# One instruction order exchanged for another in a transformer block written out by hand

## The chip, the cores and the metric

The kernel runs on one core of a Trainium2 chip. A core has a matrix engine (TensorE, PE in the profile), a vector engine (VectorE, DVE), a scalar engine (ScalarE, ACT), a small general one (GpSimd, POOL) and SyncE (SP), which here only starts transfers. Each engine works through its own list of instructions in order; between engines they wait on semaphores. On-chip memory is SBUF, and PE writes into eight PSUM banks. The metric is the device time in microseconds; three runs of the kernel before gave 239.56, 240.42 and 240.76, median 240.42.

## The reference

One block of a diffusion transformer, 2048 rows of 512 channels in bf16: a layer norm scaled and shifted by a condition, an attention in which each row sees itself and seven earlier rows two apart, a gate, and a gated feed-forward (FFN) with 1792 hidden channels.

```python
mod = (silu(c) @ w_mod).reshape(1, 6, 1, 512)
sa, ca, ga, sb, cb, gb = mod's six rows
h = layernorm(x) * (1 + ca) + sa
x = x + ga * A(h)
h = layernorm(x) * (1 + cb) + sb
x = x + gb * B(h)

def A(x):                     # 32 heads of 16, window 8, dilation 2
    q, k, v = split(x @ wqkv)
    idx = pos[:, None] - 2 * arange(8)[None, :]
    logits = einsum('bhsd,bhswd->bhsw', q, k[idx]) * 0.25    # idx < 0 masked
    return einsum('bhsw,bhswd->bhsd', softmax(logits), v[idx]) @ wo

def B(x):
    return (silu(x @ w1) * (x @ w3)) @ w2
```

## The kernel before, in words

The rows are 16 tiles T of 128. The kernel first builds a list of 1151 operations in the order of the mathematics (`_build`), each with its engine, what it reads and writes, and a key such as ("av", 3). Three tables then fix the program: `ORDER` (L1018), a permutation of the 1151 numbers; `SLOTS` (L1064), which gives each temporary value its buffer; and `place` (L147), which deals the operations of `ORDER` out to the engines, each engine keeping the sequence in which its own appear. A value that takes a buffer over also waits for all users of the one before it. `synchronize` (L169) puts the semaphore waits in and `emit` (L212) writes the five lists. So nothing is scheduled while it runs: an engine whose next instruction waits holds everything behind it. This holds for SP too, which starts nearly all transfers (L127, one line for all).

What the operations are, by line:

- **Start.** Fifteen matmuls on a tile of ones (L542) keep PE busy while loads arrive. The condition's first two rows come from matmuls with one column (L514, L517) on w_mod, which is loaded in four pieces of 256 KB: scale columns (operations 24, 25), then shift columns (26, 27). The k weights are operations 31 and 32. A small load of the w_mod corner (20) goes through ACT's queue.
- **Layer norm 1** in groups of tiles [0, 1], [2, 3], [4 to 7], [8 to 11], [12 to 15]: statistics on DVE (L580), the power -0.5 on POOL, for tiles 8 to 15 a bias on DVE (L591) and the normalising on ACT. The transposing is done by PE (L663, evicted by ACT L673), for the last group by DMA (`ln_T`, L633).
- **q, k, v.** Matmuls L722 and L749; ACT evicts them (L730, L734, L759). Each v tile goes through one of six buffers to the DRAM scratch `v_scratch_dram`.
- **Attention of a tile.** DVE multiplies q with eight shifted keys (L780, 128x4096, into a buffer of the pool "big": `sb_pq` or `sb_vsh`, later also `sb_vshx`, `sb_vshq`). PE sums over channels (L791). DVE and ACT do the softmax (L803, L808, L821, L833 to L840; L840 is a transposition on DVE). Four loads (L855) bring the shifted values from the scratch into another "big" buffer, DVE weights them (L862), PE sums over the window (L871), ACT evicts (L877), a DMA transposes (L878), PE multiplies with wo (L895) and DVE adds the residual (L899).
- **FFN** in groups of tiles [0, 1], [2, 3], [4 to 7], [8 to 11], [12 to 15], numbered 0 to 4. Layer norm 2 (`ln_sums`): mean on DVE (L610), squares on ACT (L614), POOL (L620, L621), bias on DVE (L622), normalising on ACT (L625). For groups 2 to 4 four DMA transposes (L644) and four ACT instructions (L648) then make the input h. Fourteen units of hidden channels follow, each two half units of PE (L911: w1, then w3), SiLU on ACT (L917), a copy on ACT (L921) and a product on DVE (L922), or for the last group DVE alone (L925). Then w2 (L953, L941), the residual on DVE (L969) and the store.

Weights are loaded in parts: four of w1, w3 and w2 each (operations 46 to 57; 49 is the second of w3, 54 the first of w2). The attention of later tiles is interleaved with FFN units of earlier groups, so that PE and DVE work side by side.

Of the kernel before, what the change touches and what calls it, by code (L numbers as in the profile page):

```python
# [280 lines left out]
def _build(p, A_x, A_wqkv, A_wo, B_w1, B_w3, B_w2, c, w_mod, out):  # L281
# [737 lines left out]
    15, 20, 1, 5, 7, 8, 16, 6, 17, 4, 2, 21, 58, 3, 22, 23, 28, 24, 25, 31, 32, 10, 11, 12, 13, 14, 0, 63, 64, 65, 66, 67, 87, 88, 89, 59,  # L1019
    60, 90, 68, 69, 70, 71, 92, 93, 91, 94, 61, 72, 62, 101, 19, 95, 161, 73, 163, 78, 74, 75, 79, 76, 96, 164, 162, 165, 80, 97, 102, 98,  # L1020
    77, 99, 103, 105, 115, 116, 120, 121, 106, 100, 166, 104, 107, 108, 168, 26, 81, 122, 123, 167, 169, 173, 27, 170, 82, 84, 83, 171, 174,
    176, 172, 18, 110, 127, 111, 117, 118, 125, 112, 113, 128, 126, 85, 86, 119, 124, 33, 149, 34, 35, 29, 36, 30, 37, 211, 219, 43, 38,
    212, 209, 150, 151, 217, 155, 156, 152, 157, 175, 158, 159, 153, 109, 114, 9, 180, 181, 154, 41, 49, 210, 192, 129, 195, 186, 187, 160,
    44, 198, 130, 201, 182, 218, 40, 144, 405, 220, 265, 188, 145, 45, 267, 42, 266, 139, 202, 203, 146, 147, 213, 183, 184, 140, 185, 196,
    197, 199, 404, 148, 141, 221, 193, 194, 131, 132, 133, 134, 200, 416, 214, 215, 216, 226, 225, 222, 224, 228, 223, 227, 230, 189, 177,
    233, 232, 231, 178, 234, 276, 413, 229, 274, 277, 268, 235, 415, 236, 325, 377, 142, 205, 206, 135, 179, 275, 414, 332, 334, 136, 137,
    333, 403, 190, 191, 406, 249, 251, 143, 378, 247, 253, 138, 323, 278, 269, 270, 271, 279, 273, 324, 272, 289, 280, 281, 285, 282, 207,
    208, 262, 263, 264, 248, 284, 392, 394, 393, 39, 283, 290, 291, 395, 425, 286, 287, 292, 250, 288, 294, 326, 327, 239, 240, 293, 204,
    396, 335, 397, 398, 54, 252, 243, 241, 242, 423, 237, 238, 254, 245, 295, 314, 399, 384, 259, 336, 400, 337, 338, 340, 339, 328, 401,
    297, 343, 329, 330, 341, 331, 402, 385, 417, 260, 261, 303, 299, 379, 315, 301, 380, 305, 300, 342, 52, 407, 302, 244, 246, 381, 344,  # L1030
    426, 418, 424, 304, 408, 419, 454, 420, 317, 296, 409, 427, 428, 256, 382, 386, 309, 306, 410, 320, 456, 318, 429, 430, 257, 421, 310,
    347, 422, 411, 431, 457, 455, 345, 307, 412, 639, 311, 346, 348, 387, 359, 640, 641, 642, 485, 436, 312, 643, 361, 432, 351, 446, 308,
    360, 363, 644, 646, 383, 437, 444, 298, 362, 652, 645, 255, 365, 651, 321, 653, 433, 647, 353, 447, 487, 258, 352, 354, 648, 650, 445,
    649, 371, 448, 372, 654, 368, 369, 449, 488, 450, 435, 434, 438, 486, 439, 440, 458, 459, 50, 47, 51, 316, 460, 357, 358, 355, 489, 490,
    366, 356, 491, 705, 707, 374, 364, 708, 516, 492, 493, 46, 670, 494, 313, 53, 700, 375, 715, 716, 451, 452, 453, 441, 442, 443, 733,
    349, 671, 48, 461, 462, 717, 388, 706, 350, 734, 660, 477, 735, 463, 709, 701, 718, 719, 55, 736, 737, 465, 468, 672, 467, 370, 464,
# [73 lines left out]
```

## Time and profile before

| | us |
|---|---|
| median of three runs | 240.42 |
| span of the profiled execution | 237.7 |
| PE busy | 229.9 |
| DVE busy | 169.8 |
| ACT busy | 156.4 |
| POOL busy | 23.1 |

The span runs from the first to the last instruction of the profiled execution; the time of a run also has what lies around it, 2.7 us by the difference to the median. The page has no device time of the profiled execution besides its span. PE's granted clock is at full speed in every window but the last. The transfers are heavy in the first 42 us (185 to 352 GB/s by windows of 6 us until 36 us) and light after 150 us.

### The profile page before, as it was taken

The numbers are of one execution on the slowest core, as the hardware profiler recorded it, in microseconds if no ns is written. First come the engines' busy times: TensorE is split into PE (matmuls) and PEld (weight loads), VectorE is DVE, ScalarE is ACT, GpSimd is POOL, SyncE is SP. The second block draws the span as 40 slices with busy tenths as digits, with TensorE's granted clock in tenths as the row PEclk, the third lists the DMA queues.
The fourth block names the chain that finished last, engine by engine and source line by source line (L and its number), as shares of the span: only waits on it lengthen the run. The fifth ranks groups of instructions, "written<-read, shape, count | busy, mean of one in ns | idle before, by whom it ended". The sixth has DMA issues, their size and how long they took to land.

```text
span 237.7 us, 4314 instructions
## 1 busy us (share of the span) xinstructions
PE 229.9 (97%) x1665; PEld 120.7 (51%) x1689; DVE 169.8 (71%) x284; ACT 156.4 (66%) x311; POOL 23.1 (10%) x55
## 2 busy tenths in 40 slices
PE   7899998999999999999999999999999999999996
PEld 2667543544568855754434444444344444444454
DVE  4789998999999999999999847379134424042722
ACT  2289798899989987683689799444757926133100
POOL 8323050001001000030000021000001100000000
PEclk9999999999999999999999999999999999999999
DMA  6999999989999977693897484330032142000002
GB/s 185 341 352 351 238 274 179 188 221 297 327 261 273 285 181 223 139 261 69 205 330 116 124 229 105 103 117 0 3 90 88 44 77 80 0 0 0 3 0 88
DMA packets 44731, 38.31 MB, mean 161 GB/s; under 512 B 19736, under 2 KB 36008, under 8 KB 44712
## 3 DMA queue, kind: packets, MB, share of 16 engines
q1 hardware_dynamic: 44656, 38.04, 63.3%
q8 instruction: 13, 0.21, 0.4%
q14 instruction: 6, 0.05, 0.1%
q10 hardware_dynamic: 56, 0.01, 0.0%
HBM read 29.63 MB, written 4.21 MB: 142 GB/s over the span
## 4 chain that ended last, share of the span: by engine, by line
PE 68%; DVE 12%; DMA 7%; ACT 7%; issue 3%; POOL 1%; SPq 1%; DVEq 0%
PE pall L911 38%; PE pall L953 13%; PE pall L722 5%; DMA sb_wo<-in_A_wo_dram 5%; PE pall L895 4%; DVE sb_vsh L862 3%; PE pall L941 3%; DMA sb_wm_s<-in_w_mod_dram 2%; PE pall L871 2%; PE pall L749 2%; ACT sb_h L648 1%; ACT sb_xn L614 1%; PE pall L791 1%; DVE sb_pq L780 1%; DVE sb_pq L862 1%
## 5 line engine op out<-in xcount | busy, mean ns | idle before, releaser
L911 PE MATMUL pall<-sb_h,sb_w 128*128 128x512 bf16 (+1 forms) x554 | 99.6, 336 | 0.5 <-issue 0.2
L911 PEld LDWEIGHTS pall<-sb_h,sb_w 128*128 128x128 bf16 x560 | 52.2, 98 | 47.1 <-ACT sb_sg L917 5.2
L917 ACT ACTIVATE sb_sg<-pall 128x512 bf16<-128x512 f32 (+1 forms) x70 | 33.9, 516 | 29.6 <-PE pall L911 28.6
L953 PE MATMUL pall<-sb_w,sb_hh 128*128 128x512 bf16 x190 | 43.4, 379 | 0.3
L722 PE MATMUL pall<-sb_h,sb_wqkv 128*128 128x512 bf16 (+1 forms) x157 | 30.4, 336 | 1.3 <-ACT sb_v L759 0.8
L953 PEld LDWEIGHTS pall<-sb_w,sb_hh 128*128 128x128 bf16 x196 | 18.9, 98 | 22.7 <-issue 0.4
L921 ACT ACTIVATE sb_hh<-pall 128x256 bf16<-128x256 f32 (+1 forms) x56 | 26.8, 497 | 3.4 <-PE pall L911 3.0
L922 DVE TENSOR_TENSOR sb_hh<-sb_sg,sb_hh 128x256 bf16<-128x256 bf16 (+1 forms) x56 | 17.7, 351 | 12.8 <-ACT sb_hh L921 12.8
L969 DVE TENSOR_TENSOR sb_o<-pall,sb_x 128x512 bf16<-128x512 f32 (+3 forms) x18 | 10.9, 627 | 18.5 <-PE pall L953 13.7
L722 PEld LDWEIGHTS pall<-sb_h,sb_wqkv 128*128 128x128 bf16 x160 | 14.6, 98 | 14.0 <-ACT sb_v L759 1.3
L925 DVE TENSOR_TENSOR sb_hh<-sb_sg,pall 128x512 bf16<-128x512 bf16 x14 | 9.1, 684 | 16.0 <-PE pall L911 15.9
L648 ACT ACTIVATE sb_h<-sb_h,sb_modc 128x512 bf16<-128x512 bf16 x16 | 11.7, 806 | 11.2 <-DMA sb_h<-sb_xn 11.2
L620 POOL TENSOR_SCALAR sb_rs<-sb_var 128x2 f32<-128x2 f32 x8 | 3.4, 427 | 144.4 <-ACT sb_xn L614 144.4
L862 DVE TENSOR_TENSOR sb_pq<-sb_pq,sb_al 128x4096 bf16<-128x4096 bf16 x7 | 15.8, 2285 | 1.0 <-DMA sb_pq<-v_scratch_dram 1.0
L862 DVE TENSOR_TENSOR sb_vsh<-sb_vsh,sb_al 128x4096 bf16<-128x4096 bf16 x7 | 15.9, 2281 | 0.0
L749 PE MATMUL pall<-sb_wqkv,sb_h 128*128 128x512 bf16 x59 | 15.2, 379 | 0.3 <-issue 0.2
L895 PE MATMUL pall<-sb_wo,sb_ot 128*128 128x512 bf16 x60 | 14.9, 379 | 0.6 <-issue 0.5
L673 ACT ACTIVATE sb_h<-pall,sb_modc 128x256 bf16<-128x256 bf16 (+1 forms) x20 | 12.2, 659 | 2.7 <-DVE sb_modc L522 1.8
L780 DVE TENSOR_TENSOR sb_vsh<-sb_q,sb_kT 128x4096 bf16<-128x4096 bf16 x6 | 13.6, 2286 | 0.4 <-ACT sb_q L730 0.4
L625 ACT ACTIVATE sb_xn<-sb_x,sb_nb,sb_rs 128x512 bf16<-128x512 bf16 x16 | 12.4, 818 | 1.9 <-DVE sb_nb L622 1.7
L614 ACT ACTIVATE sb_xn<-sb_x,sb_nm 128x512 bf16<-128x512 bf16 x16 | 11.4, 716 | 2.7 <-DVE sb_nm L610 2.7
L899 DVE SCALAR_TENSOR_TENSOR sb_x<-pall,sb_x 128x512 bf16<-128x512 f32 x16 | 10.7, 678 | 2.9 <-PE pall L895 2.7
(111 smaller groups left out, 254.5 us busy)
## 6 DMA issues: line engine op xcount, KB each, us to landing
sb_pq<-v_scratch_dram SPq DMA_DIRECT2D x28, 256.0 KB, 6.8
sb_vsh<-v_scratch_dram SPq DMA_DIRECT2D x28, 256.0 KB, 5.0
sb_w<-in_B_w_dram SPq DMA_DIRECT2D x6, 512.0 KB, 6.9
sb_w<-in_B_w_dram SPq DMA_DIRECT2D x6, 384.0 KB, 5.9
v_scratch_dram<-sb_v SPq DMA_DIRECT2D x16, 128.0 KB, 5.8
out_dram<-sb_o SPq DMA_DIRECT2D x14, 128.0 KB, 1.8
sb_wqkv<-in_A_wqkv_dram SPq DMA_DIRECT2D x6, 256.0 KB, 6.2
sb_x<-in_A_x_dram SPq DMA_DIRECT2D x3, 512.0 KB, 7.7
```

The costliest lines, as they stand in the source:

```text
L614: p.op("act", lambda e, vn=vn, T=T: e.activation(vn.at[:], x_sb[:, T, :], ACT.Square, bias=nm[:, T, :], scale=D ** -0.5, accum_out=var[:, ...
L648: return e.activation(vh.at[:, ft, 0:n * P], vh.at[:, ft, 0:n * P], ACT.Identity, bias=modc[:, 8 * which + ft:8 * which + ft + 1], scale=m ...
L722: ins = e.matmul(bank(vp)[:, 0:n], wqkv[:, t, kind * D + ft * P:kind * D + (ft + 1) * P], vh.at[:, t, 0:n], start=(t == ORDER[0]), stop=(t ...
L749: ins = e.matmul(bank(vp), vh.at[:, t, tt * P:(tt + 1) * P], wqkv[:, t, 2 * D:3 * D], start=(t == ORDER[0]), stop=(t == ORDER[-1]))
L780: return e.tensor_tensor(bass.AP(vp.at, 0, [[8 * D, P], [KT * P, W], [P, KT], [1, P]]), in0, in1, ALU.mult)
L862: return e.tensor_tensor(v_w, v_w, a_w, ALU.mult)
L895: ins = e.matmul(bank(vy), vt.at[:, ft, :], wo[:, ft, :], start=(ft == 0), stop=(ft == KT - 1))
L911: ins = e.matmul(bank(vp)[:, 0:n], wt[:, t, fi * P:(fi + 1) * P], vh.at[:, t, 0:n], start=(t == 0), stop=(t == KT - 1))
L917: p.op("act", lambda e: e.activation(vt.at[:, 0:n], bank(vgp)[:, 0:n], ACT.Silu), c_act(n), k, r=[vgp], w=[vt], table="silu")
L921: p.op("act", lambda e: e.activation(vh_.at[:, 0:n], bank(vup)[:, 0:n], ACT.Copy), c_act(n), k, r=[vup], w=[vh_])
L922: p.op("dve", lambda e: e.tensor_tensor(vh_.at[:, 0:n], vt.at[:, 0:n], vh_.at[:, 0:n], ALU.mult), 60 + n * 69 // 128, k, r=[vt], w=[vh_], ...
L953: ins = e.matmul(bank(vz), vhh[fi].at[:, tt * P:(tt + 1) * P], w2[:, fi, :], start=(fi == 0), stop=(fi == NF - 1))
```

## The change

The only edit is to the two tables: `ORDER` and `SLOTS` hold other numbers. All 1151 operations, each with its shape, its buffers' number and size, and each transfer stay. Beginning and end of the tables in the diff:

```diff
 ORDER = [
-    15, 20, 1, 5, 7, 8, 16, 6, 17, 4, 2, 21, 58, 3, 22, 23, 28, 24, 25, 31, 32, 10, 11, 12, 13, 14, 0, 63, 64, 65, 66, 67, 87, 88, 89, 59,
...
+    7, 6, 0, 77, 3, 76, 64, 75, 18, 69, 70, 63, 68, 72, 67, 10, 8, 1, 2, 4, 65, 23, 21, 58, 92, 93, 59, 60, 15, 9, 61, 66, 71, 24, 22, 87,
+    88, 28, 94, 95, 27, 96, 98, 102, 163, 62, 89, 11, 90, 91, 161, 5, 78, 25, 79, 80, 164, 162, 12, 165, 166, 74, 101, 97, 99, 103, 100, 26,
...
 SLOTS = [
-    0, 0, 0, 0, 0, 0, 0, 0, 0, 0, 1, 2, 2, 2, 2, 3, 0, 2, 2, 0, 1, 2, 0, 1, 0, 6, 3, 4, 3, 0, 2, 1, 5, 7, 1, 2, 0, 0, 1, 1, 1, 5, 3, 5, 6,
...
+    0, 0, 0, 0, 1, 0, 0, 0, 0, 1, 0, 5, 4, 0, 0, 0, 3, 4, 1, 1, 0, 1, 0, 2, 7, 6, 5, 0, 5, 0, 5, 4, 6, 4, 0, 1, 1, 2, 3, 2, 1, 3, 3, 6, 2,
```

Read as lists of each engine, the places that matter are these:

| | before | after |
|---|---|---|
| first loads on SP | 22, 23, 28, 24, 25, 31, 32, 26, 27 | 23, 24, 22, 28, 27, 25, 26, 31, 32 |
| matmuls on ones (L542) | nine first, six spread | eleven first, four spread |
| load 20 on ACT | first | 31st |
| v stores, values of tiles 0 and 1 on SP, in order | v1, 405, 404, 416, 413, 415, 414, 403, 406, v3, v7, v2 | v0, 403, 406, v1, 404, 405, 414, 416, 342, v2, 413, 415, 44, 343, 341, 344, v3 |
| first weightings L862 on DVE | tile 1, tile 0 | tile 0, tile 1 |
| buffer of tile 1's values | a "big" buffer not used before | that of tile 1's products |
| L840 of tiles 8 and 9, and L610 of tiles 6 and 7 | L840 first | L610 first |
| last L895 before FFN group 4 | tile 15, then tile 14, three half units, eight L953 blocks | tile 14, then tile 15, one half unit, eight L953 blocks |
| transposes of group 4 on SP | three, the store of tile 3, the fourth | all four |
| store of tile 3 | after the third transpose | before tile 15's first values |
| operation 49 (second part of w3) on SP | place 20, counted from 0 | place 63 |
| operation 54 (first part of w2) on SP | place 38 | place 60 |

The values of a tile are four loads: 403 to 406 belong to tile 0, 413 to 416 to tile 1. Operations 341 to 344 are the transposes of layer norm 1 of tiles 12 to 15, 44 is a 1 MB load of w_mod. Tiles 12 to 15's value loads also move: five of the sixteen now stand behind the store of tile 7.

113 rows, old and new, of tables (ORDER, SLOTS) are left out of this document.

## The prediction

> **What bounds the kernel now.** I read the page first, then the busy time by windows of 6 us, then the chain of waits.
>
> ```profile
> span 237.7 us, 4314 instructions
> PE 229.9 (97%) x1665; PEld 120.7 (51%) x1689; DVE 169.8 (71%) x284; ACT 156.4 (66%) x311; POOL 23.1 (10%) x55
> PE 68%; DVE 12%; DMA 7%; ACT 7%; issue 3%; POOL 1%; SPq 1%; DVEq 0%
> ```
>
> PE is busy for 97% of the span, and the chain that ended last is PE for 68%, with DVE second. No operation goes away, so only idle PE time can be won. The windows say where it lies (columns: window, us, then busy time and count of PE, weight loads, DVE, ACT, POOL; clock; DMA share; GB/s).
>
> ```profile
> 12.00:18.00 6.00, 5.82 (x52) 3.88 (x50) 4.86 (x17) 5.09 (x14) 1.64 (x4) 1.00 1.10 352
> 36.00:42.00 6.00, 5.15 (x26) 2.28 (x25) 4.99 (x4) 5.01 (x10) 0.00 (x0) 1.00 1.25 175
> 108.00:114.00 6.00, 5.95 (x76) 3.17 (x74) 6.00 (x3) 2.53 (x5) 0.00 (x0) 1.00 0.39 76
> 162.00:168.00 6.00, 5.95 (x28) 2.49 (x28) 5.06 (x4) 2.99 (x7) 0.00 (x0) 1.00 0.00 0
> ```
>
> The last row is PE at its pace: 28 matmuls 128x512 in 6 us, 0.214 us each. Four of them, a half unit of the FFN, are 0.86 us. I call **lateness** the start of an instruction less the PE work listed ahead of it, each matmul at that pace. The stretch at 36 to 42 us lost PE time; DVE is full at 108 to 114. Which wait ends last there?
>
> ```profile
> PEld pall L722 <- ACT sb_v L759: 1.0, 1, 1.0
> ACT sb_v L759 <- DMA v_scratch_dram<-sb_v: 0.8, 1, 0.8
> DVE sb_pq L862 <- DMA sb_pq<-v_scratch_dram: 1.0, 1, 1.0
> ```
>
> These are waits between 34 and 46 us (total, times, longest). PE waits for the eviction L759 of a v tile, which waits for an old v buffer to be stored; and DVE waits 1.0 us for the value loads of tile 1. The second decides more, since DVE runs almost without a gap until 133 us and so carries a lost microsecond on. Its rows, and those around FFN group 2 (tiles 4 to 7):
>
> ```profile
> 37.64 4.49 DVE L862 TENSOR_TENSOR sb_pq<-sb_pq,sb_al 128x4096 bf16<-128x4096 bf16 x2 [1.01 <-DMA sb_pq<-v_scratch_dram]
> 54.53 0.16 DVE L622 SCALAR_TENSOR_TENSOR sb_nb<-sb_sx,sb_rs 128x2 f32<-128x2 f32 x1 [0.30 <-POOL sb_rs L621]
> ...
> 103.02 0.71 DVE L840 STREAM_TRANSPOSE sb_al<-sb_attn 128x512 bf16<-128x512 bf16 x1
> 103.65 0.13 DVE L610 TENSOR_SCALAR sb_nm<-sb_sx 128x2 f32<-128x2 f32 x1
> ...
> 106.29 0.28 DVE L922 TENSOR_TENSOR sb_hh<-sb_sg,sb_hh 128x256 bf16<-128x256 bf16 x1
> 107.27 0.16 DVE L622 SCALAR_TENSOR_TENSOR sb_nb<-sb_sx,sb_rs 128x2 f32<-128x2 f32 x1 [0.70 <-POOL sb_rs L621]
> ```
>
> ```profile
> 112.94 2.93 ACT L648 ACTIVATE sb_h<-sb_h,sb_modc 128x512 bf16<-128x512 bf16 x4 [3.47 <-DMA sb_h<-sb_xn]
> ```
>
> ```profile
> 113.61 0.61 PE L791 MATMUL pall<-sb_vshq,sb_E 128*32 128x256 bf16 x16
> 114.50 0.62 PE L791 MATMUL pall<-sb_vshx,sb_E 128*32 128x256 bf16 x16 [0.28 <-DVE sb_vshx L780]
> 115.28 0.81 PE L895 MATMUL pall<-sb_wo,sb_ot 128*128 128x512 bf16 x3 [0.16 <-issue]
> 115.93 15.71 PE L911 MATMUL pall<-sb_h,sb_w 128*128 128x512 bf16 x71
> ```
>
> The mean L610 of tiles 6 and 7 starts on DVE at 103.65; squares, rstd on POOL, normalising and four DMA transposes follow, and L648 ends at 112.94 + 2.93 = 115.87. The first matmul of group 2 starts at 115.93, at once after it: this is the wait that ends last. The chain is 115.87 - 103.65 = 12.2 us long. The order lists 107.17 us of matmuls ahead of it, so its lateness is 8.75; the L791 of 113.61 has 105.4 ahead, lateness 8.2. The one other place is the start of FFN group 4:
>
> ```profile
> 182.27 1.89 PE L895 MATMUL pall<-sb_wo,sb_ot 128*128 128x512 bf16 x7
> ...
> 186.59 12.25 PE L953 MATMUL pall<-sb_w,sb_hh 128*128 128x512 bf16 x55
> 198.81 3.41 PE L911 MATMUL pall<-sb_h,sb_w 128*128 128x512 bf16 x15
> ```
>
> ```profile
> 183.99 7.14 SPq L127 DMA_TRANSPOSE sb_h<-sb_xn  x3
> 191.18 0.58 SPq L127 DMA_DIRECT2D out_dram<-sb_o  x1
> 191.80 1.20 SPq L127 DMA_TRANSPOSE sb_h<-sb_xn  x1
> ```
>
> ```profile
> DMA to landing us min/median/max: 2.3/2.3/4.0
> ```
>
> ```profile
> 195.82 2.93 ACT L648 ACTIVATE sb_h<-sb_h,sb_modc 128x512 bf16<-128x512 bf16 x4 [4.71 <-DMA sb_h<-sb_xn]
> ```
>
> Three transposes, an output store, the fourth transpose, which landed after 4.0 us where the median is 2.3; L648 ends at 198.75 and PE starts group 4 at 198.81. The 55 L953 from 186.59 are over by 186.59 + 55 x 0.214 = 198.4, so some 0.3 us are lost.
>
> **The change part by part.** It removes and adds no instruction. I count, in both lists of each engine, what stands ahead of the same operation.
>
> *Start, 0 to 14 us.* The first k matmuls need both halves of the scale columns of w_mod and the k weights. The new queue puts the shift columns (27, 26) ahead of the second scale half (25) and of wk (31, 32), one or two 256 KB pieces. At the 352 GB/s of the second window a piece is 0.75 us, so the first k matmul comes 0.7 to 1.5 us late and PE has little to put there. Some of it is recovered because the later matmuls of tiles 2 and 3 wait anyway. I take +0.4 at 14 us (bounds 0 and +1.5). It is hidden: DVE, which sets the next 100 us, had 1.01 us of wait ahead of 37.64, so it can be 0.9 later up to there and still begin its second weighting in time.
>
> *Values of tiles 0 and 1.* The new SP list issues tile 0's four loads at once and weights tile 0 first, tile 1 second. That wait is gone. But tile 1's values now take the buffer that held the products of tile 1, so their first load (414) waits for the reduction L791 of tile 1, about 30.2 us, and SP with everything behind it. Behind it stand a transpose of tile 13 (342), the store of v2, then the last two loads (413, 415), then the 1 MB load of w_mod (44). DVE finishes tile 13's bias L591 about 5 us earlier in the new list (0.1 of 24.5 us of work ahead, not 29.6), so that transpose can issue at 32 to 33, not 36.9 as the first tile's did; 1.2 us for it and 0.6 for each plain issue put the last load out at 35.2. When does it land?
>
> ```profile
> DMA to landing us min/median/max: 7.7/9.3/12.8
> ```
>
> ```profile
> DMA to landing us min/median/max: 3.4/3.4/3.4
> ```
>
> ```profile
> sb_pq<-v_scratch_dram SPq DMA_DIRECT2D x28, 256.0 KB, 6.8
> sb_vsh<-v_scratch_dram SPq DMA_DIRECT2D x28, 256.0 KB, 5.0
> ```
>
> The first row is the eight `sb_pq` loads of before in this stretch, the second one v store issued at 39.5, the others medians over the run: 3.4 to 9.3, landing 38.6 to 44.5. I take 4.6, 39.8, nearest to the 5.0 row, because about 2 MB (a w3 part, a w2 part and the w_mod part) leaves the queue ahead of these loads; at 352 GB/s that is 5.7 us less backlog. Before, the second weighting started at 37.64 + 2.20 = 39.84, with the same DVE work ahead within 0.1 us. So: **0 us**, and each microsecond of later landing costs one.
>
> *v buffers and PE at 40 us.* v stores go out before their buffers are needed, so the 1.0 us wait goes; four more matmuls stand ahead of the reduction L871 of tile 2 (+0.86), which waits for DVE. PE then has the same lateness or up to 1 us less at 62. Alone that wins nothing: group 2's h comes next.
>
> *FFN group 2.* Between the second weighting and that L610 the new DVE list holds the softmax transpose L840 no longer (start to start 103.65 - 103.02 = 0.63) and two L922 fewer on balance (0.28 each, overlapping: 0.34 with a small L622). L610 comes 0.97 us earlier; the 0.30 at 54.53 may go or stay. After it the chain of 12.2 us is the same. The same 107.17 us of PE work stands ahead of group 2's first matmul. Bounds: 0.5 (PE itself was already at 8.2 of lateness ahead of the last reduction, 8.75 - 8.2, though the stall at 40 us that is in it goes) to 1.3 (with the 0.30). I take **-1.0**. The two reductions after it wait no more: 0.86 and 1.71 us of matmuls more stand ahead of tiles 13 and 11, worth **-0.1**.
>
> *FFN group 3 and the values of tiles 12 to 15.*
>
> ```profile
> 144.10 0.17 DVE L610 TENSOR_SCALAR sb_nm<-sb_sx 128x2 f32<-128x2 f32 x1
> ```
>
> ```profile
> 152.98 2.93 ACT L648 ACTIVATE sb_h<-sb_h,sb_modc 128x512 bf16<-128x512 bf16 x4 [3.01 <-DMA sb_h<-sb_xn]
> ```
>
> From L610 to the end of L648 it took 11.8 us; with L895 (0.86) and the residual (0.7) 13.4. The new list has the last L895 before it 1.7 us later and still 14.5 us of PE work between it and the group, so h is hidden with 1 us to spare. The values' last five loads now go out behind the output store of tile 7, about 154; the four weightings (2.25 each) then end about 0.7 us before PE asks for them. I take 0 for both; what goes over costs its own length.
>
> *FFN group 4.* Between the last L895 and group 4 stand one half unit and eight L953 blocks, 13.7 us from the start of L895; before, from the second block of the 182.27 row at 183.1 to 198.8, it was two half units more, 15.7. The chain filled that, 15.6. The store is now behind the transposes: 0.62 us of issue and 4.0 - 2.3 = 1.7 of landing go, 13.3. It fits by 0.35: **-0.3**. If the 4.0 stays: 15.0 - 13.7 = 1.3 lost, so +1.3 in place of -0.3, 1.6 worse.
>
> *Weight loads.* The second w3 part (49) goes from place 20 on SP to 63 and waits there behind the transposes of tiles 2 and 3 of the attention output, about 62 us; landing at some 68 against a need at 69.4. 0, each microsecond over 1.4 costs one.
>
> *Sum.* -1.0 - 0.1 - 0.3 = -1.4: span 237.7 to 236.3. The median of three runs is 240.42, 2.7 more than the profiled span, the part outside it; with it 239.0.
>
> **A rule against the change.** The matmuls on ones:
>
> ```profile
> 1.51 4.02 PE L542 MATMUL pall<-sb_ones 128*128 128x512 bf16 x9 [1.51 <-DVE sb_ones L389]
> ```
>
> Nine take 4.02 us, 0.45 each, twice the 0.214 of later; in the window from 12 us PE works at full pace, granted clock 1.00. The new list issues eleven of them in a row and has four left to spread between the small matmuls until about 10 us, where before six filled the gaps. If PE fell back to the slow pace there, a stretch of 3 us would hold 7 such matmuls and not 14: 1.5 us lost, and DVE's products behind it as late, 239.0 + 1.5 = 240.5. The gaps of my list are near 1 us, so I give it 3 in 100. The Trainium skill, page "TensorE: Matmul & The Clock Gate", section "Why this matters for your kernels", asks for no PE gap of more than about 3 us between bursts, because an idle window brings half rate back; by that rule the sparse stretch from 7 to 10 us sits at the limit, and the trace before, with six of these matmuls in that stretch, cannot show what it does without them.
>
> **The rivals.**
> 1. *No change.* The landing of tile 1's values at 40.8 or later gives the 1.0 of group 2 back, or the fourth transpose takes 4 us whatever stands before it (239.0 + 1.6 = 240.6). For: loads of this kind took 7.7 us at the least in this stretch. Against: the backlog is shorter. 239.6 to 240.6, at 240.3.
> 2. *Slower.* SP blocks at 414 and 342, and the loads 413 and 415 issue at 36 or need the 7.7 us of before: landing at about 43.1. DVE is 3.3 us later than before's 39.84, everything up to group 2 with it, less 1.4 won: 237.7 + 3.3 - 1.4 + 2.7 = 242.3. It decides from a landing at 42.4 (239.0 + 2.6 = 241.6). For: the wait at the head of SP's queue is new. Against: half the loads land early.
> 3. *More than forecast.* The loads land at 38.9, DVE has no gap there (0.9) and none at 54.5: 239.0 - 1.2 = 237.8.
> 4. *The cold start above*, 240.5.
>
> **How the numbers follow.** About 0.5%, 1.2 us, is what a measurement of this kernel can tell from no change: faster below 239.2, slower above 241.6. Forecast, 238.3 to 239.6: 0.41, of which 0.29 is below 239.2. Rival 3: 0.16. Rival 1: 0.22. Rival 2: 0.18. Rival 4: 0.03. Faster 0.29 + 0.16 = 0.45; slower 0.18, with 0.01 of rival 4 0.19; same 0.36. The range runs from 237.6 to 242.0; half of rival 2 and a little of rival 3 lie outside. The likeliest case alone is 238.3 to 239.6.
>
> **What would show it.** No DMA wait of the first two weightings L862 and the second starting by 39.9; no wait of L759 for a store near 39; L648 of tiles 4 to 7 ending by 114.9 and group 2's matmuls right behind; three or four transposes with no store between and landings of 2.3 before group 4. The prediction is wrong if the second weighting starts after 40.5, if h of group 3 or the values of tiles 12 to 15 become waits of PE, or if a w3 load holds PE near 69 us.

## The result, and the profile after

| | before | after |
|---|---|---|
| median, us (4 runs each) | 239.99 | 242.85 |
| range of the runs | 239.48 to 240.76 | 242.30 to 244.06 |
| ratio, with 95% interval | | 1.0117 (1.0080 to 1.0154) |

The forecast was 239.0, inside 237.6 to 242.0. The changed kernel is 1.2% slower: wrong in sign and outside the range. Six more runs of it, taken later, gave 242.91 (ratio 1.0123, interval 1.0067 to 1.0179).

The page of after (its execution took 244.06 us):

```profile
span 241.5 us, 4320 instructions
PE 231.9 (96%) x1664; PEld 123.5 (51%) x1689; DVE 172.1 (71%) x284; ACT 156.6 (65%) x311; POOL 28.9 (12%) x55
PE 53%; DVE 26%; ACT 9%; DMA 5%; POOL 3%; issue 2%; SPq 1%; POOLq 0%
```

PE held 68% of the chain before and holds 53% now; DVE has gone from 12 to 26. The work is the same, so the end hangs on handovers more often. Busy time by windows, columns as in the prediction, says where:

```profile
36.00:42.00 6.00, 6.00 (x52) 2.88 (x54) 5.93 (x5) 5.33 (x10) 0.00 (x0) 1.00 1.26 241
48.00:54.00 6.00, 4.76 (x24) 1.62 (x28) 3.00 (x6) 4.58 (x9) 0.00 (x0) 0.72 0.96 282
108.00:114.00 6.00, 5.44 (x56) 2.89 (x58) 5.10 (x7) 4.43 (x10) 1.85 (x2) 1.00 0.67 151
```

The stretch that lost time before, 36 to 42 us, is full. A new hole stands at 48 to 54: PE busy 4.76 of 6 us at a mean granted clock of 0.72, with 12 matmuls of 512 columns and 12 small ones (L791), where 28 of 512 columns fill such a stretch. What was waited for between 40 and 56 us:

```profile
ACT sb_h L648 <- DMA sb_h<-sb_xn: 2.6, 1, 2.6
DVE sb_x L899 <- PE pall L895: 2.0, 2, 1.0
PE pall L722 <- ACT sb_gb_bc L571: 1.2, 1, 1.2
DVE sb_ssum L833 <- ACT pall L821: 1.0, 1, 1.0
PE pall L895 <- ACT sb_v L759: 0.7, 1, 0.7
```

The first row releases the others, as the chain of that stretch shows (start, length, what):

```profile
40.93 6.26 DMA sb_h<-sb_xn
47.20 0.02 issue
47.22 0.32 ACT sb_h L648
47.54 0.40 issue
47.94 0.57 ACT sb_gb_bc L571
48.51 0.70 ACT sb_h L648
49.22 0.13 ACT pall L821
49.35 0.29 issue
49.63 0.59 ACT sb_v L759
50.23 0.05 issue
50.27 3.40 PE pall L895 x8
```

The last DMA transpose of layer norm 1 (three are left here, of tiles 12, 14 and 15) took 6.26 us. ACT's list has its eviction L648 ahead of the small evictions L571, L821 and L759 that PE and DVE want, so one late transfer stops three engines. Then eight L895 take 3.40 us, where 1.71 is their pace: the clock has dropped to half. Why the transposes were late is in the issue times and the landings. First the load of w_mod (44), issued at 35.4, then the three transposes, issued from 37.5 to 40.9, both from the view of a tile:

```profile
DMA to landing us min/median/max: 9.0/9.0/9.0
```

```profile
DMA to landing us min/median/max: 6.3/7.2/8.7
```

The 1 MB of 44 stands in the queue ahead of them. The Trainium skill, page "DMA: Bandwidth & Descriptors", section "Queues, rings and completion order", says that an engine of the DMA consumes the descriptors of a ring in ring order; by that rule the transposes wait for 44. The landings here fit it: 44 lands at 44.3, the three at 46.3, 46.8 and 47.2.

For an overall account I take the lateness of the prediction (start less PE work ahead) at fixed amounts of work. One profiled execution of each kernel; the differences are those of the columns:

| lateness, us, after this much PE work | 35 | 50 | 69 | 100 | 224 |
|---|---|---|---|---|---|
| before (239.9 by its span and 2.2) | 6.40 | 6.97 | 7.40 | 7.86 | 10.51 |
| after (244.06) | 5.17 | 9.56 | 10.48 | 10.82 | 14.33 |
| after, again (244.02, full clock) | 5.89 | 8.82 | 10.55 | 10.55 | 14.25 |

Of the 3.8 us between the two spans, 3.8 are lost from 35 to 50 us of work (growth 4.39 against 0.57), 0.4 from 50 to 100 and 0.9 from there on, and 1.2 had been won up to 35. One such row is uncertain by about a microsecond early on: two kernels further down that are before's to the instruction up to 56 us of work show 8.7 and 8.8 there, before's own profile 7.6. The medians decide, the rows only locate. The growth from 35 to 50 us of work is steadier: every kernel measured here that keeps before's order there grows by 0.4 to 0.7, after by 4.4 and 2.9.

### The profile page after: what moved, and what is told of

Same layout as the page of the kernel before. It is cut to its first block, busy times and chain, and to the rows that moved or that the text cites. A ratio compares the mean times of both kernels' runs of the same rounds, so it can differ in the third digit from the quotient of the medians.

```text
span 241.5 us, 4320 instructions
## 1 busy us (share of the span) xinstructions
PE 231.9 (96%) x1664; PEld 123.5 (51%) x1689; DVE 172.1 (71%) x284; ACT 156.6 (65%) x311; POOL 28.9 (12%) x55
## 4 chain that ended last, share of the span: by engine, by line
PE 53%; DVE 26%; ACT 9%; DMA 5%; POOL 3%; issue 2%; SPq 1%; POOLq 0%
PE pall L911 23%; PE pall L953 12%; PE pall L722 7%; DVE sb_pq L780 4%; PE pall L895 4%; ACT sb_xn L614 3%; DVE sb_hh L922 3%; DVE sb_pq L862 3%; DVE sb_x L899 3%; DMA sb_h<-sb_xn 3%; PE pall L941 3%; DMA sb_wqkv<-in_A_wqkv_dram 2%; POOL sb_rs L620 2%; DVE sb_vshq L862 2%; DVE sb_vsh L862 2%; DVE sb_vsh L780 2%
## 5 line engine op out<-in xcount | busy, mean ns | idle before, releaser
L911 PE MATMUL pall<-sb_h,sb_w 128*128 128x512 bf16 (+1 forms) x550 | 99.9, 336 | 0.6 <-issue 0.2
L911 PEld LDWEIGHTS pall<-sb_h,sb_w 128*128 128x128 bf16 x560 | 53.7, 98 | 45.7 <-ACT sb_sg L917 1.4
L953 PE MATMUL pall<-sb_w,sb_hh 128*128 128x512 bf16 x192 | 43.4, 379 | 0.6 <-issue 0.3
L921 ACT ACTIVATE sb_hh<-pall 128x256 bf16<-128x256 f32 (+1 forms) x56 | 26.1, 498 | 8.8 <-PE pall L911 8.5
L953 PEld LDWEIGHTS pall<-sb_w,sb_hh 128*128 128x128 bf16 x196 | 18.9, 98 | 23.1 <-DVE sb_hh L922 1.0
L620 POOL TENSOR_SCALAR sb_rs<-sb_var 128x2 f32<-128x2 f32 x8 | 5.4, 675 | 151.7 <-ACT sb_xn L614 151.7
L922 DVE TENSOR_TENSOR sb_hh<-sb_sg,sb_hh 128x256 bf16<-128x256 bf16 (+1 forms) x56 | 17.2, 350 | 5.2 <-ACT sb_hh L921 3.3
L648 ACT ACTIVATE sb_h<-sb_h,sb_modc 128x512 bf16<-128x512 bf16 x16 | 11.9, 805 | 12.0 <-DMA sb_h<-sb_xn 12.0
L895 PE MATMUL pall<-sb_wo,sb_ot 128*128 128x512 bf16 x62 | 17.0, 407 | 0.8 <-ACT sb_v L759 0.7
L862 DVE TENSOR_TENSOR sb_pq<-sb_pq,sb_al 128x4096 bf16<-128x4096 bf16 x7 | 16.0, 2286 | 1.3 <-DMA sb_pq<-v_scratch_dram 1.2
L780 DVE TENSOR_TENSOR sb_pq<-sb_q,sb_kT 128x4096 bf16<-128x4096 bf16 x7 | 16.0, 2280 | 0.0
L780 DVE TENSOR_TENSOR sb_vsh<-sb_q,sb_kT 128x4096 bf16<-128x4096 bf16 x7 | 15.8, 2272 | 0.0
L862 DVE TENSOR_TENSOR sb_vsh<-sb_vsh,sb_al 128x4096 bf16<-128x4096 bf16 x5 | 11.4, 2285 | 3.3 <-DMA sb_vsh<-v_scratch_dram 3.3
```

The lines of the kernel that those rows point to most:

```text
L780: return e.tensor_tensor(bass.AP(vp.at, 0, [[8 * D, P], [KT * P, W], [P, KT], [1, P]]), in0, in1, ALU.mult)
L862: return e.tensor_tensor(v_w, v_w, a_w, ALU.mult)
L895: ins = e.matmul(bank(vy), vt.at[:, ft, :], wo[:, ft, :], start=(ft == 0), stop=(ft == KT - 1))
L911: ins = e.matmul(bank(vp)[:, 0:n], wt[:, t, fi * P:(fi + 1) * P], vh.at[:, t, 0:n], start=(t == 0), stop=(t == KT - 1))
L921: p.op("act", lambda e: e.activation(vh_.at[:, 0:n], bank(vup)[:, 0:n], ACT.Copy), c_act(n), k, r=[vup], w=[vh_])
L922: p.op("dve", lambda e: e.tensor_tensor(vh_.at[:, 0:n], vt.at[:, 0:n], vh_.at[:, 0:n], ALU.mult), 60 + n * 69 // 128, k, r=[vt], w=[vh_], ...
```

## The experiments

The theory after the result was that **the hole behind load 44** costs the 2.9 us. The rivals: the **start** (reordered loads, bunched matmuls on ones), and the **late part** (group 2, where I had counted a gain, or waits of DVE for POOL). Kernels measured together share the runs of before, whose median was 239.6 to 240.2. Numbers in the diffs are operations in an engine's list.

**1. Load 44 behind the transposes (in after).**

```diff
 SP: 413, 415,
-    44, 343, 341, 344
+    343, 341, 344, 44
```

> The changed kernel, with one move on SP: the 1 MB load of w_mod (44) goes behind the transposes of tiles 12, 14 and 15 (343, 341, 344) that stood behind it. Theory Q (the transposes land 6.3 to 8.7 us after issue because the 1 MB is ahead of them, and L648, heading ACT's list, then holds the evictions that PE needs): they land in 2.5 to 4 us, ACT waits for them under 0.8 us in place of 2.6, the PE gaps at 47 and 49 us go, and the time falls by 2 to 3 from 242.85, to 240 or 240.5, unless the matmuls on that w_mod part (L497) now wait for it. Theory I (the transposes are late because SP issues the last at 40.9, after ACT's normalising): landings stay near 47, no change, 242.5 to 243.

245.31, ratio 1.021 (1.0158 to 1.0262): worse. The transposes landed soon:

```profile
DMA to landing us min/median/max: 2.4/3.0/3.8
```

Those are the landings of the three. But 44, now issued at 44.8 and landing at 50.7, stood ahead of a transpose of the attention output, which took 6.2 us and kept PE's L895 waiting (lateness 7.8, then 10.3). The delay behind 44 is shown, and that another transfer now takes it. That the edit makes the kernel slower than after is not shown: three of the four executions (245.20, 245.42, 246.36) have a mean clock of 0.986 to 0.993, and the profiled one is at half from 10.1 to 13.5 us, before the place that was edited, and already some 2 us behind after there. The only one at full clock took 243.43.

**2. ACT's small evictions first (in after).** The evictions L648 of two tiles (345, 347) go behind those that PE and DVE want.

```diff
 ACT: 
-    345, 387, 347, 429, 318, 321, 308
+    387, 429, 318, 321, 308, 345, 347
```

> The changed kernel with all transfers as they are; only on ACT the four L648 of tiles 12 to 15 go behind the eviction L571, the exponential L821 and the evictions of v10, v11 and q14 that stood behind or between them. If it is the place at the head of ACT's list that stops PE (part two of theory Q), the transposes still land near 47 but PE's gaps at 47 and 49 us go, and 2 to 2.8 us with them: about 240.3. If PE needs h of tiles 12 to 15 itself at that time, the wait moves to L722 of tile 16's columns and under 1 us is won: 242 or more.

242.99, ratio 1.0113 (1.0077 to 1.0150). The wait of ACT for the transposes went, and the time stayed. In the profiled execution the clock was at half from 8.6 to 12.0 us, behind a gap of 1.29 us in which PE waited for load 25; it ran some 2 us late from there on, and the transposes landed after 4.5 to 5.3 us, so the wait did not go by the edit alone. The three executions at full clock took 241.50, 241.66 and 243.09, the three with a half-clock dip 242.89, 243.34 and 243.99; three are too few to tell 241.66 from after's full-clock executions, whose median is 242.7.

**3. Load 44 early (in after).**

```diff
 SP:
-    414, 416, 342, 204, 413, 415, 44
+    44, 414, 416, 342, 204, 413, 415
```

> The changed kernel, with the 1 MB load (44) moved ahead of the first value load of tile 1 (414), where SP stands idle from 24 to 30.4 us. Theory Q: the load is over by about 34, the transposes land in under 4 us, L497 has its weights early, the hole at 47 to 54 us goes whole: 239.5 to 240.2, so at or below the kernel before, and below it by the 1.4 of my prediction if its other steps hold (238.6). Theory I: 242.5 to 243. If the value loads of tile 1 suffer by it, the second weighting starts after 40.5 in place of 39.6.

242.90, ratio 1.0126 (1.0089 to 1.0162). The hole is gone, the transposes land in 3.2 to 4.0 us, but 44 now stands ahead of the values (the waits from 34 to 62 us):

```profile
DVE sb_vsh L862 <- DMA sb_vsh<-v_scratch_dram: 0.9, 1, 0.9
```

Lateness at 50 us of work falls from 9.56 to 7.03, at 69 it is 9.34 again: on the way PE waits 0.36 us for a normalising (58.8), and 0.80 at 78.0 ahead of an L911 whose part of w3 lands at 77.9. Taking the hole out gained nothing.

**4. Group 2's mean first (in before).** My -1.0 by itself: L610 of tiles 6 and 7 (835) ahead of L840 (526).

```diff
 DVE:
-    526, 835
+    835, 526
```

> The kernel before with one exchange on DVE: the mean L610 of tiles 6 and 7 ahead of the softmax transpose L840, as in the changed order. My step for FFN group 2: L610 0.63 us earlier, h of group 2 0.6 us earlier, the first L911 of the group at 115.3 in place of 115.9; 0.5 to 0.6 us faster, ratio 0.9975. The rival: L840, 0.1 us later, and the product of tile 13 set PE at 114.5 anyway, and the time stays within 0.2.

240.60, ratio 1.0021 (1.0001 to 1.0042), 12 runs against 17 of before: no gain. PE's timeline at the last reductions and the start of group 2:

```profile
114.89 0.61 PE L791 MATMUL pall<-sb_vshq,sb_E 128*32 128x256 bf16 x16
115.78 0.62 PE L791 MATMUL pall<-sb_vshx,sb_E 128*32 128x256 bf16 x16 [0.28 <-DVE sb_vshx L780]
116.33 1.04 PE L895 MATMUL pall<-sb_wo,sb_ot 128*128 128x512 bf16 x4
117.20 5.13 PE L911 MATMUL pall<-sb_h,sb_w 128*128 128x512 bf16 x23
```

PE waits for the product L780 ahead of the last L791, and then runs into group 2 without a wait for h. h had been one of two chains that end within a few tenths of each other.

**5 and 6. One order up to 70 us, then the other.** The first 480 operations of before, then after's sequence (ten slots moved); and the first 468 of after, then before's.

```diff
-ORDER = after                     # 5
+ORDER = first 480 of before, then the rest as in after
-ORDER = before                    # 6
+ORDER = first 468 of after, then the rest as in before
```

> The first 480 operations in the old order (on the engines to about 63 to 70 us), then the rest in the new one; slots follow, with ten temporary values in other buffers so that no wait is cyclic. Theory A (what is lost arises before 57 us: start, hole at 47 to 54, and the normalising of tiles 0 and 1 behind it): lateness of PE near 7.6 at 66 us as before, and the time 239 to 240.3, with whatever the new later part wins. Theory B (the loss is spread, and the later part costs as much through its own small waits): 241 to 241.5.

> The first 468 operations in the new order (to about 68 us), the rest in the old one; four values in other buffers. Theory A: 242 to 243, like the changed kernel. Theory B: 241 to 241.5. If the two halves add, this and the other hybrid together miss the kernel before by what the changed kernel misses it, 2.6 to 2.9 us.

245.08 (1.0191, 1.0151 to 1.0230) and 251.10 (1.0446, 1.0389 to 1.0502). Both lose at the seam, because loads that one order expects early the other issues late; in the second, PE waited for a part of w3 (its waits from 60 to 85 us):

```profile
PE pall L911 <- DMA sb_w<-in_B_w_dram: 4.5, 1, 4.5
```

All six executions of run 6 also fall to half clock behind that wait (mean clock 0.986 to 0.993). So the totals don't separate the halves. What can be used is the growth of lateness from 100 to 224 us of work, behind the seam: 3.65 with after's late part, 2.50 with before's (after 3.51, before 2.65).

**7 and 8. Where before has its loads (in after).** Load 20 first on ACT, 44 at the place at which before has it (issued at 21.1 here), 46 later on SP; and the same with the first 140 operations in before's order.

```diff
 ACT:
+    20
     21, 58, 99, ...
-    133, 20
+    133
 SP:
+    44
     40, 404,
-    46
...
     413, 415,
-    44
     343, 341, 344, 208, 52, 410, 258, 420
+    46
```

> The changed kernel; on ACT's queue the small load 20 is first again, on SP the 1 MB load 44 goes behind the store of v1, as in the old order (issued near 22 us), and the 0.5 MB weight load 46 goes from there to behind the transpose 420, about 47 us, 15 us ahead of its use. So nothing large stands ahead of tile 1's values or of the transposes. Theory A: second weighting by 40, transposes within 4 us, no hole, 1.5 to 2.5 us faster than the changed kernel: 240.3 to 241.2 (what is left being the start and the later waits). If the hole cost little by itself: 242.5.

> As the kernel before it in this list, and the first 140 operations of the old order ahead (to about 16 us: loads, matmuls on ones, first k matmuls). If the start costs 0.5 to 1 us and its jitter, as the lateness of 5.0 against 5.2 to 6.9 says: 239.5 to 240.3, level with the kernel before; if the start is hidden, as I predicted, no more than 0.2 faster than the one without it.

243.26 (1.0117, 1.0081 to 1.0154) and 242.70 (1.0104, 1.0072 to 1.0136). In the first, the profiled execution was the fastest of ten (241.42): lateness 7.05 at 50, 8.27 at 100, 11.69 at the end, so there the early loss was gone and the late one left. The other nine were slower, up to 246.49 (two of them, 244.80 and 246.49, with a mean clock of 0.993), and have no profile. In the second, at 50 us of work lateness is before's (7.01), and then the values of tile 3 are late, as DVE's timeline shows:

```profile
60.73 2.29 DVE L862 TENSOR_TENSOR sb_pq<-sb_pq,sb_al 128x4096 bf16<-128x4096 bf16 x1 [2.07 <-DMA sb_pq<-v_scratch_dram]
```

At 56 us of work it is 10.0. With the start and the hole both repaired, the next transfer takes their place. The two differ by the start alone, and by 0.56 us, of which 0.36 lies outside the span (see Open); the intervals overlap.

**9 and 10. After again, and with before's start.** After unaltered; and with its first 140 operations in before's order.

```diff
-ORDER = after                     # 10
+ORDER = first 140 of before, then the rest as in after
```

> The changed kernel once more, unaltered, for a second profile and more executions. Theory A+ (two things raise it: a hole behind the transposes near 48 us in each execution, and in some a stretch of 3.4 us at half clock, at the start or in the hole, about 1.7 us): 242 to 243 with clock 1.0, near 244 where the mean clock reads 0.993, about one in four; the new profile shows ACT's wait for the transposes again. If the hole was an accident of the first profile, its lateness at 50 us is near 7 in place of 9.6.

> The changed kernel with the first 140 operations in the old order (to about 16 us), all else as in the changed one, the place of the 1 MB load too. Theory A+: no execution with clock 0.993 from the start any more, spread as narrow as the old order's, median 0.3 to 0.8 below the changed one (242.0 to 242.5); the hole near 48 us remains. If the start decides nothing: the same median and the same share of low clocks as the changed kernel.

242.91 (1.0123, 1.0067 to 1.0179) and 242.91 (1.0122, 1.0065 to 1.0179): undoing the start alone did not lower the time. The profile of the first, at full clock, has the hole again:

```profile
ACT sb_h L648 <- DMA sb_h<-sb_xn: 2.8, 1, 2.8
PE pall L722 <- ACT sb_gb_bc L571: 1.3, 1, 1.3
PE pall L895 <- ACT sb_v L759: 0.7, 1, 0.7
```

So the hole doesn't come from the half clock; that adds to it. In the second, lateness goes from 5.7 to 7.1 between 10 and 20 us of work, which neither parent shows: this seam loses time of its own, so the run can't say what the start costs in after. The two profiles of after put it low: at 20 us of work their lateness is 5.06 and 5.79, before's 5.09.

**11. After's start in before.** The first 125 operations in after's order, two slots moved.

```diff
-ORDER = before
+ORDER = first 125 of after, then the rest as in before
```

> The other way round: the kernel before with the first 125 operations in the new order (two temporary values in other PSUM banks). Theory A+: some executions (a fifth to a half) read 0.993, with a stretch at half clock near 8 to 14 us, and are 1 to 1.7 us longer; the median rises by 0.3 to 1. If the low clock belongs to the later part of the changed kernel: all read 1.0 and the time is that of the kernel before within 0.4.

242.15, ratio 1.0111 (1.0055 to 1.0167). The start alone costs before some 2.6 us, 0.36 of it outside the span. Two of the six executions (243.78, 244.06) have a mean clock of 0.993; the other four have a median of 241.86.

**12. POOL's waits apart (in after).** The theory for the late part was that L622 waits on DVE for POOL, and holds a product up. The products 487 and 549 go ahead of it.

```diff
 DVE:
-    644, 487, ..., 840, 549
+    487, 644, ..., 549, 840
```

> The changed kernel; on DVE the products of tiles 7 and 11 (L780) change places with the bias L622 just ahead of them, which waited 0.9 and 1.0 us for POOL. Theory P (POOL's L620 stands still while DVE runs a 128x4096 product or weighting, 1.1 to 2 us in place of 0.22, and DVE then waits for POOL): DVE loses 1.5 us less by 114 us, and the lateness at 107 us falls by 0.8 to 1.5; time 0.5 to 1.2 less than the changed kernel's. If h of the groups, which now comes 1.3 us later, sets PE instead: no change or slower.

250.71 by the median of four, ratio 1.0433 (1.0360 to 1.0506): one took 489.02 us, the others 249.44, 250.47 and 250.96. L622 now comes a product later, so normalising and PE's transposes wait (PE's timeline):

```profile
63.05 0.29 PE L663 MATMUL pall<-sb_ident,sb_xn 128*128 128x128 bf16 x2 [1.29 <-ACT sb_xn L625]
```

The kernel is 8 us slower than after, where 0.5 to 1.2 were to be gained. In all three the clock fell to half as well (in the profile from 51.2 to 54.6 and from 64.9 to 68.3), so the 8 us are not all the exchange's own. The wait for POOL is the cheaper of the two orders.

**13. After's order from 80 us on.** The first 588 operations of before, seven slots moved.

```diff
-ORDER = after
+ORDER = first 588 of before, then the rest as in after
```

> The first 588 operations in the old order (to about 80 us), then the new one; seven temporary values in other buffers. All three gains of my prediction (group 2 -1.0, tile 11 -0.1, group 4 -0.3) lie in the part that is new here. If they hold: 238.2 to 238.8 where the kernel before takes 239.7. If the later part costs by itself, as the lateness says that grows by 3.5 from 100 us on in place of 2.65: 240.3 to 240.8, with the matmul L791 of tile 11 waiting 0.7 us for its product, and DVE for POOL.

246.03, ratio 1.0251 (1.0211 to 1.0291). At 114.25 PE waits 2.40 us for a product, and the half clock follows (114.3 to 117.7 us; five of the six executions have a mean clock of 0.993); part of that product's delay comes from the slots that had to move, so this run sizes nothing.

**14 and 15. The two parts of the start (in before).** The first eleven loads in after's order; and eleven matmuls on ones first.

```diff
 SP:                               # 14
-    22, 23, 28, 24, 25, 31, 32, 26, 27, 33, 34
+    23, 24, 22, 28, 27, 25, 26, 31, 32, 34, 33
 PE:                               # 15
-    61, 72, 101, 73
+    72, 73, 61, 101
```

> The kernel before with only the first eleven loads on SP in the new order (shift columns of w_mod ahead of the second scale half and of wk); PE, DVE and all else as before. If the load order is what the new start costs: first k matmuls 0.7 to 1.5 us late, some executions at clock 0.993, median 241 to 242. If it is the matmuls on ones: 239.7 to 240.2, all clocks 1.0.

> The kernel before with only the matmuls on ones moved: eleven in a row at first and four spread, as in the new order, where before nine and six. If thin filling lets the clock fall: a fifth or more of the executions at 0.993, those 1.7 us longer, median up by 0 to 0.6. If the clock needs the later loads too (a gap of 1.3 us as in the profile of the second experiment): all at 1.0 and 239.7 within 0.3.

241.82 (1.0082, 1.0052 to 1.0113) and 239.65 (0.9998, 0.9972 to 1.0023), 12 runs each. The loads cost 2.3 us, the bunching nothing. What the loads did, by windows of 1 us of the first:

```profile
5.00:6.00 1.00, 0.15 (x1) 0.00 (x1) 0.93 (x5) 0.00 (x0) 0.53 (x3) 1.00 0.79 249
6.00:7.00 1.00, 0.50 (x2) 0.19 (x2) 0.97 (x4) 0.00 (x0) 0.70 (x2) 1.00 1.00 317
7.00:8.00 1.00, 0.88 (x14) 0.55 (x14) 1.00 (x5) 0.00 (x0) 0.73 (x2) 1.00 0.89 313
8.00:9.00 1.00, 1.00 (x12) 0.40 (x11) 0.90 (x5) 0.00 (x0) 0.11 (x1) 0.53 0.97 323
9.00:10.00 1.00, 1.00 (x8) 0.63 (x6) 0.39 (x2) 0.17 (x1) 0.92 (x3) 0.50 1.00 350
```

PE is sparse for 2 us (0.15 and 0.50), and the clock is at half from 8 us. But only five of the twelve executions have this dip; their median is 242.01, that of the other seven 241.68. So most of the 2.3 us is there without the dip: the late loads themselves.

**16. Two weights later (in before).** The w3 part 49 moved from place 20 on SP to 37, the w2 part 54 behind 53.

```diff
 SP:
-    49, 160, 44, ..., 204, 54, 343, ..., 313, 53
+    160, 44, ..., 204, 49, 343, ..., 313, 53, 54
```

> The kernel before with two weight loads later on SP: the second part of w3 (49) from place 20 to where the first of w2 (54) stood, near 30 us, and 54 behind the last w3 part, near 60 us. 0.5 MB less ahead of tile 1's values: at 352 GB/s they land 1.4 us earlier, the 1.0 us wait of the first weighting goes, DVE is 0.9 earlier until 130 us, time 0.4 to 0.9 less: 238.9 to 239.4. If other loads fill the queue anyway: no change; if 54 lands after its scaling on DVE at 71 us needs it: slower by that wait.

241.38, ratio 1.0058 (1.0026 to 1.0091). Lateness at 56 us of work is 6.61 where before has 7.63, which is within the microsecond by which such rows differ, so an early gain is not shown. What shows is the time, and two waits later on, of PE and of DVE (their timelines):

```profile
67.92 1.90 PE L895 MATMUL pall<-sb_wo,sb_ot 128*128 128x512 bf16 x8 [1.42 <-DMA sb_ot<-sb_oa]
75.61 1.23 DVE L996 TENSOR_TENSOR sb_w<-sb_w,sb_gb_bc 128x2048 bf16<-128x2048 bf16 x1 [0.93 <-DMA sb_w<-in_B_w_dram]
```

**17 and 18. Group 4's transposes together (in before).** The store 826 behind the fourth transpose 1065; and this with the matmuls of run 15.

```diff
 SP:                               # 17 and 18
-    826, 1065
+    1065, 826
 PE:                               # 18 only
-    61, 72, 101, 73
+    72, 73, 61, 101
```

> Before with one thing of the change: on SP the output store of tile 3 (826) behind the fourth transpose of group 4 (1065). My term for group 4 (0.62 us of issue and 1.7 of landing go): the fourth transpose issues at 191.2, not 191.8, and lands after 2.3 us, h of group 4 ends some 2 us earlier, PE starts group 4 about 0.3 us earlier, 0.3 us less than before in the span (239.3 where before is 239.6). Rival, that the landing of 4.0 comes from the transposes standing back to back and not from the store between them: it lands after 3.5 to 4 us as in the changed kernel, h ends at most 0.6 earlier; the same 0.3 us of wait can go by that alone. Rival, that nothing here binds: ratio 1.000.

> Before with the two edits that so far cost nothing: eleven matmuls on ones first and four spread (as b3), and the store of tile 3 behind the fourth transpose. If the terms add, 239.3 where before is 239.6 (ratio 0.998 to 1.000), and it is the best version that these experiments point to; if neither binds, ratio 1.000 within 0.3%.

239.96 (0.9978, 0.9947 to 1.0009) and 239.55 (0.9980, 0.9950 to 1.0009), where before has 240.17; in the second, one execution, the profiled one, took 833 us. Both intervals hold 1, so no version here is shown to beat before. SP and the landing in the first:

```profile
185.03 8.44 SPq L127 DMA_TRANSPOSE sb_h<-sb_xn  x4
```

```profile
DMA to landing us min/median/max: 2.3/2.3/4.2
```

The four go out with no store between them, and the longest still takes 4.2 us: the store was not what made the fourth slow. From 170 us of work to the end lateness grows by 0.57, in before by 0.72.

## Why the prediction was wrong

**What failed.** The step "Values of tiles 0 and 1" followed SP's list as far as load 44 and stopped there: "then the 1 MB load of w_mod (44)". Behind it stand three transposes, 343, 341 and 344, which I listed in the table of the change and costed nowhere, though by my own words I counted, in both lists of each engine, what stands ahead of the same operation. In after they land 6.3 to 8.7 us after their issue, and at that place the kernel loses 2.9 us from 35 to 50 us of work at full clock (lateness 5.89 to 8.82), where before loses 0.57. "PE then has the same lateness or up to 1 us less" under "v buffers and PE at 40 us", set at 0, is the term in which this belonged. Taking the hole out did not bring the time back (runs 1, 3, 7 and 8), so how much of the final 2.9 us is the hole's own stays open. A smaller slip: the 2.7 us outside the span set a median against the span of one execution. Where time and span belong to the same execution, before has 2.2, so the forecast stood 0.5 too high by this term; after has 2.57.

**What was right and didn't help.** The two rows of DVE that were to decide, in after:

```profile
37.40 2.29 DVE L862 TENSOR_TENSOR sb_pq<-sb_pq,sb_al 128x4096 bf16<-128x4096 bf16 x1
39.60 2.28 DVE L862 TENSOR_TENSOR sb_vsh<-sb_vsh,sb_al 128x4096 bf16<-128x4096 bf16 x1
```

No DMA wait, and the second weighting at 39.60 where 39.8 was forecast. Rival 2, the slow one, was about these values. It did not happen; the loss came 8 us later from the same queue. The 1.0 us wait of L759 for a store went, as forecast.

**Start, +0.4, "It is hidden".** The delay is there: in before the loads alone cost 2.3 us (run 14), the whole start 2.6 (run 11). What it costs in after is open: undoing it left the time as it was, but lost time at its own seam (run 10), and at 20 us of work after is at most 0.7 behind before. I had put the cover on DVE's 1.0 us wait ahead of 37.64; the price in before, 2.3 to 2.6, was larger than my bound of 1.5.

**FFN group 2, -1.0.** Mis-sized: it is worth 0 or less. PE's and ACT's timeline in after:

```profile
113.36 0.62 PE L791 MATMUL pall<-sb_vshx,sb_E 128*32 128x256 bf16 x16 [0.56 <-DVE sb_vshx L780]
...
119.46 8.79 PE L911 MATMUL pall<-sb_h,sb_w 128*128 128x512 bf16 x39
```

```profile
115.69 2.93 ACT L648 ACTIVATE sb_h<-sb_h,sb_modc 128x512 bf16<-128x512 bf16 x4 [2.25 <-DMA sb_h<-sb_xn]
```

h is there at 118.62 (115.69 + 2.93), 0.84 ahead of its first use, so the chain that I shortened no longer ends last. In its place PE waits for DVE's product, 0.56 us. Run 4 shows the same in before's own order: the mean 0.6 earlier, the time no shorter. My lower bound of 0.5 took the lateness ahead of the last reduction as PE's own, but that was DVE's product already: DVE stands behind both chains, and moving one operation of it ahead makes another later.

**Tiles 13 and 11, -0.1.** The wait is 0.56 in after, not shorter than before's 0.28.

**Group 3, values of tiles 12 to 15, weight loads: 0 each.** No wait for h of group 3 or for the values of tiles 12 to 15 shows as a loss: from 126 to 170 us of work lateness grows by 0.91, in before by 0.76. The weight load cost something: in the second profile of after PE waits 0.7 us for a part of w3 at 79, later than the 69.4 that I watched.

**Group 4, -0.3.** Half right. The chain was to end earlier by 0.62 of issue and 1.7 of landing; the landing did not shrink (4.2 in run 17, 3.9 in after), and by the profile of run 17 0.15 is won (0.72 less 0.57), with a ratio that fits -0.3 and 0 alike. In after, lateness grows by 0.87 from 170 on, and h still ends last (timelines of PE and ACT):

```profile
190.27 12.49 PE L953 MATMUL pall<-sb_w,sb_hh 128*128 128x512 bf16 x55
202.71 3.63 PE L911 MATMUL pall<-sb_h,sb_w 128*128 128x512 bf16 x16
```

```profile
199.72 2.93 ACT L648 ACTIVATE sb_h<-sb_h,sb_modc 128x512 bf16<-128x512 bf16 x4 [3.86 <-DMA sb_h<-sb_xn]
```

The L953 (56 by the list, one has no record) are over by 190.27 + 56 x 0.214 = 202.25. L648 ends at 202.65, and PE starts group 4 at 202.71: some 0.5 us are lost, against 0.3 by the same working in before.

**The rest.** Rival 4 had the right mechanism in the wrong place and too small a chance: the clock does fall to half in these kernels, but behind the new load order (run 14) and the hole, not with the bunched matmuls (run 15, twelve executions with none).

**Why repairing one thing never helped.** Four places were each seen to lose 0.7 to 3 us: the loads of the start, the transposes behind 44, the values of tile 3, parts of w3. Removing one (runs 3, 7, 10) or two (run 8) left the time at 242.7 to 243.3 (run 1, at 245.3, has the half clock in three of its four executions). In runs 3, 8 and 16 the profile shows the next transfer that then came late. That they all pass through SP's one list is the reading that fits, but it is not a matter of bytes alone: in before the DMA engines are busy at 0.89 to 1.25 in every window of 6 us from 6 to 84 us, while in after their share falls to 0.69 from 30 to 36 us and to 0.37 from 66 to 72, where SP stands at a transfer that waits (24.1 to 30.5 ahead of load 414; two transposes of the attention output until 69.7) with loads of w behind it. Neither part was tested, by taking bytes away or by clearing SP's list.

**Open.** The 0.8 to 1.0 us from 100 us of work on returns in every kernel with after's late part (growth 3.4 to 4.0 against 2.5 to 2.7; runs 12 and 13, with losses of their own there, are left out), and I can't divide it. By the figures above 0.15 of after's 0.86 arise from 126 to 170 us of work and 0.15 from 170 on, so the larger part, some 0.5, lies between 100 and 126: the waits for DVE's product at 113 and for POOL are candidates, and the one trial (run 12) failed by its own cost. The times of all runs with after's first 125 operations stand 2.57 us above their spans, those with before's first operations 2.2 to 2.3. This 0.36 us outside the span is not from the order of the first loads or the bunched matmuls (2.20 and 2.21), nor from the place of load 20, which run 7 has first again (2.52 to 2.62); its cause was not found.

## What to carry to other kernels

When a large load is moved in a queue, follow the list beyond it to the next small transfer that an engine waits for, and then that engine's own list: with 1 MB ahead of three transposes the kernel lost 2.9 us at that place, twice the forecast gain of 1.4, though taking it out did not give the time back. Where two chains end within some tenths of each other, shortening one is worth those tenths only; look for the second one first. Where many transfers share one list, an order found by removing the visible wait has only chosen which transfer is late, so it is to be judged by the time and not by the wait that went.

## What the runs showed of the hardware

**Half clock after short gaps.** PE gaps of 0.85 and 0.62 us with little between them (run 14), or of 1.29 us (run 2), were followed by 3.4 us at a granted clock of 0.50, as long as the stretch in after (50.5 to 53.9 us). The Trainium skill, page "TensorE: Matmul & The Clock Gate", section "Why this matters for your kernels", warns of gaps of more than about 3 us; the gaps here are less than half of that, so the sparse stretch as a whole may count; which of the two does was not tested. Executions of one kernel differ: 5 of 12 in run 14, 2 of 10 of after. Of the 101 executions of before with a clock on record none has a mean below 0.999.

**POOL stands still beside DVE.** The power L620 on 128 x 2 numbers, grouped by line, first in after, then in before (ns, least, median, most):

```profile
L620 POOL TENSOR_SCALAR sb_rs<-sb_var x8: 217/217/1951, 56.2 to 193.1; 128x2 f32<-128x2 f32 x8
```

```profile
L620 POOL TENSOR_SCALAR sb_rs<-sb_var x8: 217/400/904, 53.2 to 187.6; 128x2 f32<-128x2 f32 x8
```

The same instruction takes 217 ns, or 1951. The long one and what DVE ran beside it:

```profile
56.24 1.95 POOL L620 TENSOR_SCALAR sb_rs<-sb_var 128x2 f32<-128x2 f32 x1 [25.57 <-ACT sb_xn L614]
```

```profile
55.86 2.25 DVE L780 TENSOR_TENSOR sb_vsh<-sb_q,sb_kT 128x4096 bf16<-128x4096 bf16 x1
```

It ends at 58.19, just after the product ends at 58.11. In after again an L620 of 1.14 us ends at 110.11, beside a weighting L862 that ends at 110.04. The Trainium skill, page "SBUF — State Buffer", section "SBUF: two separate sides", says that a DVE operation with two SBUF inputs and a GpSimd operation that reads SBUF, as L620 does, exclude each other for a whole instruction; by that rule POOL waits for the product, and these rows agree. My estimate from them: a small POOL operation between two DVE operations costs up to the length of the product beside it, and one that starts 0.4 us after such a product, as here, takes 1.7 longer (1951 less 217 ns).
